# An attention and expert kernel: one written list for all engines, three score banks, output by transposition

## The chip, the cores and the metric

The kernel runs on one core of one Trainium2 chip. The metric is device time in microseconds, from a median of several runs. The core has five engines that matter here, each with its own instruction queue, executed in order: TensorE (PE in the profile; its weight loads have a lane of their own, PEld), VectorE (DVE), ScalarE (ACT), GpSimd (POOL), and SyncE (SP), which issues most DMA. TensorE writes only to PSUM, which has eight banks of 128 x 512 float32; DVE and ACT read it.

## The reference, cut to what matters

```python
# attention: B=8, H=8, S=576, D=64, window 128, per head an ALiBi slope
scores = q @ k.T / 8 + slope[h] * -(i - j)      # kept where 0 <= i - j < 128, else -1e9
attn   = exp(scores - max); attn /= sum + 1e-9
x      = (attn @ v) as (4608 tokens, 512)
# experts: N=4608, D=512, E=8, F=1024, capacity 576 tokens each
logits = x @ w_gate                             # 512 x 8
# tokens are assigned greedily in order of falling logit, 576 to each expert
out[mask_e] = relu(x[mask_e] @ w1[e]) @ w2[e]
```

## The kernel before, in words

The program has two stages. Attention fills the first 215 us of the span, the router and the eight experts the rest. The change touches attention alone.

Attention works on 32 pairs of heads (`NPAIRS = B * NP`, four pairs a batch of 576 tokens). Queries go in blocks of 64, and two neighbouring blocks and the two heads of the pair share a unit `t`, so a pair has five units, 0 to 4, the last a half one. Units 2 and 3 make up "half 0" of the scores, units 0, 1 and 4 "half 1" (`UNITS`). Even batches start their blocks at another place than odd ones: `unit()` gives unit 0 two key blocks and unit 4 three in even batches, and three and one in odd ones. So rounds come in two kinds, four of one and four of the other.

A pair passes through these steps, all of whose instructions are kept in the order of the program text by `put`, on every engine:

- `scores(n, half)`: TensorE in 64 x 64 tiles writes q k of a half into two banks, one per head. Products in plain float32 take two passes, each with its own weight load.
- `least(n, half)`: DVE adds the bias, stores the weights' exponents to `u` and their minimum to `mn`.
- `exps(n, half)`: ACT takes the exponential in place and sums it to `sm`.
- `turn(n, t, ps)`: TensorE transposes `u` into a bank (128 x 128, one pass; unit 4 is done with 64 x 64 products and goes into unit 0's bank); `turned` copies the bank to `PT0` to `PT3`, by ACT (units 2 and 0) or DVE (1 and 3).
- `av(n)`: TensorE in 64 x 64 tiles makes the transposed output x in two banks.
- `copy_out(n)`: ACT copies them to `xT`; POOL adds 1e-9 to the sums (`sd`).
- `natural(n, N)`: for each of five 128-token groups one product of `xT` (as weights, 128 x 128) with `wn`, which has 144 columns: an identity of 128 that turns x to token-major, and 16 gate columns, for the logits.
- `divide(n, N)`: DVE takes the reciprocal of the sums, then for each of two banks multiplies the 16 columns into `Lp` (`shares`) and the 128 into `xb` (`output`); SP stores `xb`; once a batch `logits` adds on POOL.

The loop runs 36 rounds. Round n works on five pairs at once: in TensorE's order it turns units 2, 1, 3 of pair n-2, makes `natural` of pair n-4, turns units 0 and 4 of pair n-2, makes `scores(n, 0)`, `av(n-3)` and `scores(n, 1)`. Between them `router.early_step` puts small pieces of the router (TensorE and DVE).

PSUM is split by pools: `ps_s` two banks (scores), `ps_t` four (turned weights and `natural`), `ps_x` two (`av`). A bank is given out in turn, and its next writer waits for the last reader of what was in it. A round takes four score banks: each half waits for `least` of the other half to have read both.

In the text below T0 to T4, S0, S1, A and N stand for TensorE's part of those steps, M for an instruction of `least`, E of `exps`, P0 to P3 for the copies of `turned`, X for the copies of `copy_out`.

Of the kernel before, what the change touches and what calls it, by code (L numbers as in the profile page):

```python
# [21 lines left out]
LAG = 2  # L22
UNITS = (2, 3), (0, 1, 4)
QKW, BMW, XW = 1152, 1216, 144


def attention(tc, pools, qk_in, v_in, rel_in, C, x_dram, L_sb, router):
# [18 lines left out]
    ident, wn = C["ident"], C["wn"]  # L46
# [59 lines left out]

    def scores(n, half):
        st = state[n]
# [12 lines left out]
        st["s"] = s  # L121

    def least(n, half):

        st = state[n]
        s = st["s"]
        for t in UNITS[half]:
            for h in range(2) if t < 4 else (0,):
                m, c, _, y = unit(n, t)
                y += 512 * h  # L130
                i = 2 * t + h
                u = weights(n, t, h)
                for rows, x in ((slice(0, 128), s[h]),) if t < 4 else ((hs[0], s[0]), (hs[1], s[1])):
                    put(nc.vector.tensor_tensor_reduce(out=u[rows], in0=x[rows, c:c + 64 * m].rearrange("q (j k) -> q j k", k=64),  # L134
                                                       in1=bm[n % NP][rows, y:y + 64 * m].rearrange("q (j k) -> q j k", k=64),
                                                       scale=-0.125, scalar=3e38, op0=ALU.add, op1=ALU.min,
                                                       accum_out=st["mn"][rows, i:i + 1]))

    def exps(n, half):
        st = state[n]  # L140
        for t in UNITS[half]:
            for h in range(2) if t < 4 else (0,):
                i = 2 * t + h
                u = weights(n, t, h)
                put(nc.scalar.activation(u, u, AF.Exp, bias=st["mn"][:, i:i + 1], scale=-1.0, accum_out=st["sm"][:, i:i + 1]))  # L145
# [5 lines left out]
    def turn(n, t, ps):  # L151

        u = state[n]["u"]
        m, _, o, _ = unit(n, t)
        for j in range(m):
            c = place(n, t, j)
            if t < 4:
                put(nc.tensor.transpose(ps[:, c:c + 128], u[:, o + 128 * j:o + 128 * j + 128], ident))  # L158
            else:
                for h in range(2):  # L160
                    mm(ps[hs[h], c:c + 64], u[hs[h], o + 64 * j:o + 64 * j + 64], ident[hs[h], hs[h]])

    def turned(n, t, ps, copy):
        T = state[n][t] = sb.tile([128, 576], F32, name=f"PT{t}")
        w = 384 if t else place(n, 4, unit(n, 4)[0])
        put(copy(T[:, 0:w], ps[:, 0:w]))
# [43 lines left out]
    def copy_out(n):  # L210
        st = state[n]
        xT = st["xT"] = sb.tile([128, 576], F32, name="xT")
        for i, w in ((0, 320), (1, 256)):
            put(nc.scalar.copy(xT[:, 320 * i:320 * i + w], st["x"][i][:, 0:w]))
# [17 lines left out]
    def divide(n, N):  # L232

        b, p = divmod(n, NP)
        bb, par = divmod(b, 2)
        if p == 0:
            batch[b] = (sb.tile([128, 5, 512], F32, name="xb", bufs=2), sb.tile([128, 5, 8, 8], F32, name="Lp", bufs=2))
        xb, Lp = batch[b]
        s = sb.tile([128, 5, 2], F32, name="rs")
        put(nc.vector.reciprocal(s, state.pop(n)["sd"].rearrange("q (t h) -> q t h", h=2)))  # L240

        def views(i):
            t0, t1 = (0, 3) if i == 0 else (3, 5)
            return t0, t1, N[i][:, 0:XW * (t1 - t0)].rearrange("q (t c) -> q t c", c=XW)

        def shares(i):
            t0, t1, x = views(i)
            put(nc.vector.tensor_tensor(Lp[:, t0:t1, :, 2 * p:2 * p + 2].rearrange("q t e h -> q t h e"),
                                        x[:, :, 128:144].rearrange("q t (h e) -> q t h e", h=2),
                                        bc(s[:, t0:t1].unsqueeze(3), [128, t1 - t0, 2, 8]), ALU.mult))  # L250

        def output(i):
            t0, t1, x = views(i)
            if n < NPAIRS - 2:
                put(nc.vector.tensor_tensor(xb[:, t0:t1, 128 * p:128 * p + 128].rearrange("q t (h c) -> q t h c", h=2),
                                            x[:, :, 0:128].rearrange("q t (h c) -> q t h c", h=2),
                                            bc(s[:, t0:t1].unsqueeze(3), [128, t1 - t0, 2, 64]), ALU.mult))
            else:
                for t in range(t0, t1):
                    for h in range(2):  # L260
                        put(nc.scalar.mul(xb[:, t, 128 * p + 64 * h:128 * p + 64 * h + 64],
                                          x[:, t - t0, 64 * h:64 * h + 64], s[:, t, h:h + 1]))

        def store():
            c0, cs = 9 * bb + 5 * par, 9 * bb + 4
# [3 lines left out]
            if p == NP - 1:  # L269
                nc.sync.dma_start(x_dram[128 * cs + 64 * par:128 * cs + 64 * par + 64, :], xb[hs[par], 4, :])  # L270

        for i in range(2):
            shares(i)
            if n < NPAIRS - 2:
                output(i)
# [8 lines left out]
        else:  # L284
            store()

# [26 lines left out]
    def bank():  # L313
        return ps_t.tile([128, 512], F32, name="pt")

    for n in range(NPAIRS + LAG + 2):
# [4 lines left out]
        if n == 2:  # L321
            nc.sync.dma_start(wn, C["wn_in"])
# [4 lines left out]
        k = n - LAG  # L327
        turns, ends = 0 <= k < NPAIRS, 0 <= k - 2 < NPAIRS
        if ends:
            copy_out(k - 2)  # L330
        if 0 < n <= NPAIRS:
            least(n - 1, 1)
        if turns:
            ps = {}
            for t in (2, 1, 3):
                ps[t] = bank()
                turn(k, t, ps[t])
            turned(k, 2, ps[2], nc.scalar.copy)
        if 0 < n <= NPAIRS:
            exps(n - 1, 1)  # L340
        if turns:
            turned(k, 1, ps[1], nc.vector.tensor_copy)
            turned(k, 3, ps[3], nc.vector.tensor_copy)
            room = ps[3][:, 384:512]
        if k - 1 == NPAIRS - 1:
            av(k - 1)
        if ends:
            N = [bank(), bank()]
            natural(k - 2, N)
        if turns:  # L350
            ps = bank()
            turn(k, 0, ps)
            turn(k, 4, ps)
            turned(k, 0, ps, nc.scalar.copy)
        if n < NPAIRS:
            if ends:

                router.early_step(room)
            scores(n, 0)
            least(n, 0)  # L360
            exps(n, 0)
        if ends:
            divide(k - 2, N)
            if (k - 2) % NP == NP - 1 and k - 2 < NPAIRS - 1:
                logits((k - 2) // NP)
        if 0 <= k - 1 < NPAIRS - 1:
            av(k - 1)
        if n >= NPAIRS:
            for _ in range(1 if turns else 2):
                router.early_step(room if turns else bank()[:, 384:512])  # L370
        if n < NPAIRS:
            scores(n, 1)


def host_attn(inputs):
# [9 lines left out]
    wn = np.zeros((2, D, NP, 2, XW), np.float32)  # L385
    for c in range(2):
        for o in range(2):
            h = c ^ o
            for d in range(D):
                wn[c, d, :, o, D * h + d] = 1.0  # L390
            wn[c, :, :, o, 128 + 8 * h:136 + 8 * h] = g[:, h].transpose(1, 0, 2)
# [7 lines left out]
    for r in range(2):  # L399
# [5 lines left out]
        for p in range(NP):  # L405
            rel[r, :, 512 + p] = 2.0 ** -(2 * p + r + 1)
    return dict(qk=qk.reshape(B, NP, 128, QKW), v=np.ascontiguousarray(vv).reshape(B, NP, 128, NB * D),
                wn=wn.reshape(128, 2 * NP * XW),
# [848 lines left out]
def moe_attn_kernel(tc, qk, v, w1, w2, wn, rel, ident, cst, out):  # L1257
    nc = tc.nc
    with ExitStack() as es:
# [4 lines left out]
        C = dict(ident_in=ident, wn_in=wn, cst_in=cst)  # L1264
# [6 lines left out]
        with ExitStack() as ea:  # L1271
            P["pp"] = ea.enter_context(tc.tile_pool(name="pp", bufs=1))
            P["attn"] = ea.enter_context(tc.tile_pool(name="attn", bufs=2))
            for k, b in (("ps_s", 2), ("ps_t", 4), ("ps_x", 2)):
                P[k] = ea.enter_context(tc.tile_pool(name=k, bufs=b, space=PSUM))
            warm(tc, P, C)
            C["wn"] = P["pp"].tile([128, 2 * NP * XW], F32, name="wn_sb")
# [17 lines left out]
_INS = ["qk", "v", "w1", "w2", "wn", "rel", "ident", "cst"]  # L1295
# [23 lines left out]
```

## Time and profile before

| what | value |
|---|---|
| median of three runs | 683.64 us (681.84, 684.50, 683.64) |
| the profiled execution | 683.86 us, of which the span of the trace is 681.7 us |
| PE, PEld busy | 655.0 us (96%), 580.3 us (85%) |
| DVE, ACT, POOL busy | 468.5, 386.4, 134.2 us |
| granted TensorE clock | 0.985 on average |
| `scores` of pair 5 to pair 31 (26 rounds) | 31.83 to 198.16 us |

A line of the timeline has the start and the length in us, the engine, the line of the kernel, the operation, what it writes and reads, and how many instructions of that kind were merged. A matmul's length contains a fixed latency, so in a stream the starts tell more than the lengths. PE rows of line 54 are the helper `mm`: their tiles say which step they belong to (`s<-qk` scores, `x<-PT,v` A, `pt<-wn_sb,xT` N, `pt<-ident_sb,u` 64*64 is T4); line 158 is T0 to T3, line 134 M, 145 E, 166 P, 214 X, 248 and 255 `shares` and `output`.

### The profile page before, as it was taken

What the parts mean: (1) busy time and instruction counts of PE and PEld (TensorE: products, weight loads), DVE (VectorE), ACT (ScalarE), POOL (GpSimd) and SP (SyncE); (2) the same over time, 40 slices, a digit from 0 to 9 for tenths busy, and PEclk for the clock granted to TensorE, in tenths of its full rate; (3) what the DMA queues carried; (4) which work ended last, traced back from release to release, by engine and by line L of the source; (5) the groups of instructions that cost most, each with busy time, mean ns of one, the idle gap of its engine ahead of it and who ended that gap; (6) DMA issues with size and microseconds to landing.
All of it is one profiled execution on the core that took longest, in us unless ns stands there. A gap on an engine that the chain in (4) does not pass through costs nothing.

```text
span 681.7 us, 18901 instructions
## 1 busy us (share of the span) xinstructions
PE 655.0 (96%) x7152; PEld 580.3 (85%) x7152; DVE 468.5 (69%) x1985; ACT 386.4 (57%) x1091; POOL 134.2 (20%) x296
## 2 busy tenths in 40 slices
PE   7999999999996699999999999999999999999995
PEld 4998998998986399889779879989989989989985
DVE  5788888888887799979749879776756625423210
ACT  6998898898884162434224546455546645644210
POOL 4021121121121201421412124013014014011011
PEclk9999999999998699999999999999999999999999
DMA  8556566566532361814515736637546556421001
GB/s 304 155 180 203 180 181 205 178 185 201 179 101 76 99 220 53 295 39 155 178 47 198 191 115 214 130 100 228 111 116 201 137 119 201 124 70 39 1 25 50
DMA packets 58980, 98.65 MB, mean 145 GB/s; under 512 B 27648, under 2 KB 36992, under 8 KB 58880
## 3 DMA queue, kind: packets, MB, share of 16 engines
q1 hardware_dynamic: 52992, 78.48, 38.6%
q0 software_dynamic: 5888, 18.88, 8.4%
q8 instruction: 58, 0.95, 0.6%
q14 instruction: 42, 0.34, 0.2%
HBM read 72.57 MB, written 18.87 MB: 134 GB/s over the span
## 4 chain that ended last, share of the span: by engine, by line
PE 86%; DVE 8%; DMA 3%; issue 1%; ACT 1%; POOL 0%; SPq 0%; POOLq 0%; DVEq 0%; ACTq 0%
PE ph L1059 24%; PE po L1087 10%; PE po L1088 10%; PE s L54 9%; PE po L1090 8%; PE pt L54 7%; PE pt L158 7%; PE x L54 6%; DMA raw<-in_w_dram 2%; DVE hl L967 2%; DVE hlo L1069 1%; PE m L610 1%; DVE u L134 1%; PE pg L1000 1%; PE ph L984 1%
## 5 line engine op out<-in xcount | busy, mean ns | idle before, releaser
L1059 PE MATMUL ph<-xh,hl 128*128 128x288 f32 (+2 forms) x1024 | 188.3, 298 | 0.6 <-ACT hh L1064 0.5
L1059 PEld LDWEIGHTS ph<-xh,hl 128*128 128x128 f32 x1024 | 154.6, 189 | 2.1 <-ACT hh L1064 0.7
L145 ACT ACTIVATE u<-u,mn 128x192 f32<-128x192 f32 (+2 forms) x288 | 123.9, 433 | 24.5 <-DVE mn L134 24.5
L1087 PE MATMUL po<-hl,hh 128*128 128x512 f32 (+1 forms) x328 | 128.3, 391 | 0.0
L1088 PE MATMUL po<-hl,hh 128*128 128x512 f32 (+1 forms) x328 | 126.2, 385 | 0.0
L1059 PE MATMUL ph<-xl,hl 128*128 128x288 f32 (+2 forms) x512 | 115.5, 297 | 0.0
L134 DVE CUSTOM_DVE_ANT_0 u<-s,bm 128x192 f32<-128x192 f32 x308 | 86.5, 333 | 30.0 <-PE s L54 29.2
L1064 ACT ACTIVATE hh<-ph 128x288 fp32r<-128x288 f32 (+2 forms) x128 | 46.5, 408 | 106.3 <-PE ph L1059 103.1
L1090 PE MATMUL po<-hl,hlo 128*128 128x512 f32 (+1 forms) x264 | 101.3, 384 | 0.0
L967 DVE TENSOR_TENSOR hl<-raw,hl 128x512 fp32r<-128x512 f32 x128 | 85.1, 684 | 22.0 <-ACT hl L965 21.6
L1099 POOL DMA_INDIRECT out_dram<-o,idx x40 | 42.2, 1056 | 274.9 <-ACT o L1094 216.0
L1059 PEld LDWEIGHTS ph<-xl,hl 128*128 128x128 f32 x512 | 84.1, 189 | 0.2 <-DVE xl L1038 0.2
L965 ACT CAST hl<-raw 128x1024 fp32r<-128x1024 f32 x64 | 65.9, 1051 | 22.1 <-DMA raw<-in_w_dram 17.7
L54 PE MATMUL s<-qk 64*64 64x192 f32 (+1 forms) x1112 | 69.7, 319 | 1.9 <-DVE mn L134 1.6
L1069 DVE SCALAR_TENSOR_TENSOR hlo<-ph,hh 128x288 fp32r<-128x288 f32 (+2 forms) x128 | 49.1, 416 | 32.5 <-ACT hh L1064 31.9
L1087 PEld LDWEIGHTS po<-hl,hh 128*128 128x128 f32 x328 | 61.8, 188 | 11.2
L1088 PEld LDWEIGHTS po<-hl,hh 128*128 128x128 f32 x328 | 61.7, 188 | 11.3
L1094 ACT COPY o<-po 128x512 f32<-128x512 f32 (+1 forms) x33 | 18.9, 573 | 91.0 <-PE po L1090 80.8
L1090 PEld LDWEIGHTS po<-hl,hlo 128*128 128x128 f32 x264 | 49.7, 188 | 9.9
L158 PE MATMUL pt<-ident_sb,u 128*128 128x128 f32 x368 | 54.2, 282 | 1.4 <-DVE mn L134 1.0
L54 PEld LDWEIGHTS s<-qk 64*64 64x64 f32 x1112 | 48.3, 132 | 8.1 <-issue 2.5
L145 ACT ACTIVATION_READ_ACCUMULATOR u<-u,mn 128x1 f32 x288 | 54.4, 189 | 0.0
(240 smaller groups left out, 902.6 us busy)
## 6 DMA issues: line engine op xcount, KB each, us to landing
raw<-in_w_dram SPq DMA_DIRECT2D x64, 512.0 KB, 4.3
qk<-in_qk_dram SPq DMA_DIRECT2D x32, 576.0 KB, 5.1
v<-in_v_dram SPq DMA_DIRECT2D x32, 288.0 KB, 3.6
x<-xb SPq DMA_DIRECT2D x14, 512.0 KB, 3.5
x<-xb SPq DMA_DIRECT2D x8, 128.0 KB, 3.2
x<-xb SPq DMA_DIRECT2D x4, 256.0 KB, 2.3
g<-x,idx POOLq DMA_INDIRECT x40, 3.8
out_dram<-o,idx POOLq DMA_INDIRECT x40, 2.8
```

Of the source, the lines that this page charges most:

```text
L54: put(nc.tensor.matmul(out, w, a, start=start, stop=stop, skip_group_check=True))
L134: put(nc.vector.tensor_tensor_reduce(out=u[rows], in0=x[rows, c:c + 64 * m].rearrange("q (j k) -> q j k", k=64), in1=bm[n % NP][rows, y:y ...
L145: put(nc.scalar.activation(u, u, AF.Exp, bias=st["mn"][:, i:i + 1], scale=-1.0, accum_out=st["sm"][:, i:i + 1]))
L158: put(nc.tensor.transpose(ps[:, c:c + 128], u[:, o + 128 * j:o + 128 * j + 128], ident))
L965: self.last = nc.scalar.copy(hl[:, 0, :], raw)
L967: nc.vector.tensor_tensor(hl[:, 1, c:c + 512], raw[:, c:c + 512], hl[:, 0, c:c + 512].bitcast(F32), ALU.subtract)
L1059: nc.tensor.matmul(pp[t], w[:, a, j, fo:fo + 128], x[:, j, cut[t]:cut[t + 1]], start=(i == 0), stop=(i == 11))
L1064: self.acted = nc.scalar.activation(o, pp[t], AF.Relu)
L1069: nc.vector.scalar_tensor_tensor(d, pp[t][:, c0:c1], 0.0, o[:, c0:c1].bitcast(F32), ALU.max, ALU.subtract)
L1087: nc.tensor.matmul(out, a, wh, start=(f == 0), stop=False)
L1088: nc.tensor.matmul(out, a, wl, start=False, stop=(f == 7 and t == 4))
L1090: nc.tensor.matmul(out, hl[:, f, 128 * t:128 * t + 128], wh, start=False, stop=(f == 7))
```

## The change

The order of a round is written out in one list, `ROUND`, whose entries are a step, its unit or half, and how many rounds back its pair started. The list orders each engine's work; instructions of different engines still wait only for data and buffers. `least`, `exps`, `turn`, `turned`, `copy_out`, `natural` and `divide` now do one unit, half or parity per call. Read by engine, the list is:

- PE: T0, S0, A, T4, S1, (router), T2, N odd, T1, N even, T3
- ACT: E00, E20, E40, E21, P3, E10, X1, E11, X0, E30, E01, P1, E31
- DVE: M11, D even, M30, M20, M21, reciprocal, (router), P0, M31, M01, P2, D odd, M10, M00, M40
- POOL: the sums (G)

The score pool has three banks and the pool of turned weights three. The turning goes by 128 x 128 transposition in `natural`, and a product with 16 columns (`wg`) makes the logits; groups are taken by the parity of t, and odd ones have their two heads swapped, so that `output` of the odd groups takes two instructions. P0 and P2 are on DVE, P1 and P3 on ACT. `sums` and the reciprocal are steps of their own. The last pair's `av` follows its P0 at once.

```diff
-LAG = 2
 UNITS = (2, 3), (0, 1, 4)
-QKW, BMW, XW = 1152, 1216, 144
+QKW, BMW, XW, GW = 1152, 1216, 144, 16
+ROUND = [(w[0], w[1:-2], int(w[-1])) for w in (
+    "T0-2 S0-0 E00-1 M11-1 De-4 E20-1 E40-1 G-2 A-3 E21-1 M30-0 P3-2 E10-1 M20-0 M21-0 X1-3 I-3 E11-1 T4-2 S1-0 R-0 T2-1 P0-2 "
+    "M31-0 X0-3 M01-0 No-3 E30-0 T1-1 P2-1 E01-0 Do-3 M10-0 M00-0 M40-0 P1-1 Ne-3 T3-1 E31-0").split()]
+ROUNDS = 4
...
-        s = [bank() if half and n < 2 else ps_s.tile([128, 512], F32, name="s") for _ in range(2)]
+        s = st["s", half] = [bank() if half and n == 0 else ps_s.tile([128, 512], F32, name="s") for _ in range(2)]
...
-    def turn(n, t, ps):
+    def turn(n, t):
+        ps = state[n]["pt", t % 4] = state[n]["pt", 0] if t == 4 else bank()
...
-    def turned(n, t, ps, copy):
+    def turned(n, t):
+        copy = nc.scalar.copy if t % 2 else nc.vector.tensor_copy
+        put(copy(T[:, 0:w], state[n]["pt", t][:, 0:w]))
+        if t == 0 and n == NPAIRS - 1:
+            av(n)
...
-    def natural(n, N):
-        for t in range(5):
-            w = xT[:, places[t]:places[t] + 128]
-            c = 2 * (n % NP) + t % 2
-            mm(N[t // 3][:, XW * (t % 3):XW * (t % 3) + XW], w, wn[:, XW * c:XW * c + XW])
+    def natural(n, par):
+        par = "eo".index(par)
+        N = state[n]["N", par] = bank()
+        g = GW * (2 * (n % NP) + par)
+        for i, t in enumerate(range(par, 5, 2)):
+            w = xT[:, places[t]:places[t] + 128]
+            put(nc.tensor.transpose(N[:, XW * i:XW * i + 128], w, ident))
+            mm(N[:, XW * i + 128:XW * i + XW], w, wg[:, g:g + GW])
...
+            elif a == 0:
+                put(nc.vector.tensor_tensor(xb[:, ts, 128 * p:128 * p + 128].rearrange("q t (h c) -> q t h c", h=2), ...
             else:
+                for h in range(2):
+                    put(nc.vector.tensor_tensor(xb[:, ts, 128 * p + 64 * h:128 * p + 64 * h + 64],
+                                                x[:, :, 64 - 64 * h:128 - 64 * h],
+                                                bc(s[:, ts, h:h + 1], [128, m, 64]), ALU.mult))
...
+        if par:
+            return
         (store and logits as before, after the even groups)
...
+    def route(n):
+        for _ in range(1 if n < NPAIRS + 2 else 2):
+            if n >= 4:
+                router.early_step(state[n - 2]["pt", 3][:, 384:512] if n < NPAIRS + 2 else bank()[:, 384:512])
+    for n in range(NPAIRS + ROUNDS):
+        (loads as before; wg, 128 columns, in place of wn, 1152)
+        for what, which, back in ROUND:
+            k = n - back
+            if what == "R":
+                route(n)
+            elif 0 <= k < NPAIRS:
+                ...
-            for k, b in (("ps_s", 2), ("ps_t", 4), ("ps_x", 2)):
+            for k, b in (("ps_s", 3), ("ps_t", 3), ("ps_x", 2)):
```

More of the change, by code (lines that the diff above doesn't have):

```diff
@@ L120, in scores, with least @@
                 mm(s[h][hs[r], c:c + w], q[hs[h], 64 * qb:64 * qb + 64], k[hs[h], 64 * kb:64 * kb + w])
-        st["s"] = s
-    def least(n, half):
+    def least(n, which):
+        t, h = int(which[0]), int(which[1])
         st = state[n]
[L126 to L137, printed above, removed]
@@ L139, in exps @@
-    def exps(n, half):
-        st = state[n]
[L141 to L145, printed above, removed]
+        s = st["s", int(t not in UNITS[0])]
+        m, c, _, y = unit(n, t)
+        y += 512 * h
+        i = 2 * t + h
+        u = weights(n, t, h)
+        for rows, x in ((slice(0, 128), s[h]),) if t < 4 else ((hs[0], s[0]), (hs[1], s[1])):
+            put(nc.vector.tensor_tensor_reduce(out=u[rows], in0=x[rows, c:c + 64 * m].rearrange("q (j k) -> q j k", k=64),
+                                               in1=bm[n % NP][rows, y:y + 64 * m].rearrange("q (j k) -> q j k", k=64),
+                                               scale=-0.125, scalar=3e38, op0=ALU.add, op1=ALU.min,
+                                               accum_out=st["mn"][rows, i:i + 1]))
@@ L208, in av, with copy_out, sums @@
                     mm(out, w, a, i == 0, i == len(todo[hc]) - 1)
[L210 removed]
+    def copy_out(n, i):
         st = state[n]
[L212 to L214 removed]
+        i = int(i)
+        if "xT" not in st:
+            st["xT"] = sb.tile([128, 576], F32, name="xT")
+        c, w = ((0, 320), (320, 256))[i]
+        put(nc.scalar.copy(st["xT"][:, c:c + w], st["x"][i][:, 0:w]))
+    def sums(n):
+        st = state[n]
         st["sd"] = sb.tile([128, 10], F32, name="sd")
@@ new lines, in output @@
+        def output(a):
+            ts, m, x = views(a)
+            if n >= NPAIRS - 2:
+                for i in range(m):
+                    t = a + 2 * i
+                    for h in range(2):
+                        o = 64 * (h ^ a)
+                        put(nc.scalar.mul(xb[:, t, 128 * p + 64 * h:128 * p + 64 * h + 64], x[:, i, o:o + 64], s[:, t, h:h + 1]))
+            elif a == 0:
+                put(nc.vector.tensor_tensor(xb[:, ts, 128 * p:128 * p + 128].rearrange("q t (h c) -> q t h c", h=2),
@@ L269, in store @@
             if p == NP - 1:
[L270 to L275, printed above, removed]
+                nc.sync.dma_start(x_dram[128 * cs + 64 * odd:128 * cs + 64 * odd + 64, :], xb[hs[odd], 4, :])
+        shares(par)
+        if n < NPAIRS - 2:
+            output(par)
+        if par:
+            return
         if n == NPAIRS - 2:
@@ L311, in attention, with values @@
     biases(0)
-    def bank():
-        return ps_t.tile([128, 512], F32, name="pt")
-    for n in range(NPAIRS + LAG + 2):
+    def values(n):
+        if n < NPAIRS - 1:
+            av(n)
+    def route(n):
+        for _ in range(1 if n < NPAIRS + 2 else 2):
+            if n >= 4:
+                router.early_step(state[n - 2]["pt", 3][:, 384:512] if n < NPAIRS + 2 else bank()[:, 384:512])
+    work = dict(S=scores, M=least, E=exps, T=turn, P=turned, X=copy_out, N=natural, D=divide)
+    alone = dict(A=values, G=sums, I=inverse)
+    for n in range(NPAIRS + ROUNDS):
         if 0 < n < NPAIRS - 1:
@@ L326, in attention @@
             biases(n)
[L327 to L372, printed above, removed]
+        for what, which, back in ROUND:
[3 more added lines that the diff above has]
+            elif 0 <= k < NPAIRS:
+                if what in alone:
+                    alone[what](k)
+                else:
+                    work[what](k, which)
 def host_attn(inputs):
```

75 lines of the change are left out of this document (41 added, 34 removed).

## The prediction

> **What bounds the kernel now.** I read the page first (busy shares, slices), then busy time by stage, then TensorE's timeline of one round of each kind.
>
> ```profile
> span 681.7 us, 18901 instructions
> PE 655.0 (96%) x7152; PEld 580.3 (85%) x7152; DVE 468.5 (69%) x1985; ACT 386.4 (57%) x1091; POOL 134.2 (20%) x296
> PEclk9999999999998699999999999999999999999999
> 6.00:31.83 25.83, 22.70 (x428) 19.03 (x428) 21.35 (x123) 23.56 (x100) 8.39 (x29) 1.00 0.73 246
> 31.83:198.16 166.33, 166.21 (x3430) 150.07 (x3426) 136.70 (x736) 144.30 (x575) 32.05 (x154) 1.00 0.59 182
> ```
>
> The last two lines are start:end, length, and busy time of PE, PEld, DVE, ACT and POOL (the stretches run from the first scores to those of pair 5, and from there to those of pair 31). In the second PE is busy 166.21 of 166.33 us: 26 rounds at 6.40 us, bound by TensorE, with DVE at 82% (5.26 a round) and ACT at 87% (5.55). In the first, ACT leads. But a busy PE is not one at its peak, so its own timeline decides.
>
> ```profile
> 111.33 1.20 PE L158 MATMUL pt<-ident_sb,u 128*128 128x128 f32 x9
> 112.37 1.39 PE L54 MATMUL pt<-wn_sb,xT 128*128 128x144 f32 x10
> 113.70 0.44 PE L158 MATMUL pt<-ident_sb,u 128*128 128x128 f32 x2
> 114.06 0.51 PE L54 MATMUL pt<-ident_sb,u 64*64 64x64 f32 x10
> 114.46 0.82 PE L54 MATMUL s<-qk 64*64 64x192 f32 x14
> 115.05 1.56 PE L54 MATMUL x<-PT,v 64*64 64x64 f32 x64
> 116.53 1.37 PE L54 MATMUL s<-qk 64*64 64x128 f32 x20
> 117.83 0.55 PE L158 MATMUL pt<-ident_sb,u 128*128 128x128 f32 x3
> ...
> 143.30 1.20 PE L158 MATMUL pt<-ident_sb,u 128*128 128x128 f32 x9
> 144.34 1.39 PE L54 MATMUL pt<-wn_sb,xT 128*128 128x144 f32 x10
> 145.64 0.55 PE L158 MATMUL pt<-ident_sb,u 128*128 128x128 f32 x3
> 146.11 0.27 PE L54 MATMUL pt<-ident_sb,u 64*64 64x64 f32 x2
> 146.83 1.60 PE L54 MATMUL x<-PT,v 64*64 64x64 f32 x64
> 148.34 1.26 PE L54 MATMUL s<-qk 64*64 64x192 f32 x20
> 149.54 0.33 PE L158 MATMUL pt<-ident_sb,u 128*128 128x128 f32 x1
> ```
>
> From start to start, an even batch's round is T2, T1, T3 1.04, N 1.33, T0 0.36, T4 with S0 0.99, A 1.48, S1 1.30: 6.50 us. An odd one's is 1.04, 1.30, 0.47, 0.72, 1.51, 1.20: 6.24. Mean 6.37. Two of these hold waits. The first is S1's:
>
> ```profile
> 115.46 0.36 DVE L134 CUSTOM_DVE_ANT_0 u<-s,bm 128x192 f32<-128x192 f32 x1 [1.35 <-PE s L54]
> 116.30 0.35 DVE L134 CUSTOM_DVE_ANT_0 u<-s,bm 128x192 f32<-128x192 f32 x1
> 116.49 0.19 PEld L54 LDWEIGHTS s<-qk 64*64 64x64 f32 x2
> 116.77 0.77 PEld L54 LDWEIGHTS s<-qk 64*64 64x64 f32 x18
> ```
>
> With two score banks, S1 may write only when the four M of S0 (first and last shown, 115.46 to 116.65) have read both banks. Two of its 20 loads go at 116.49, the other 18 at 116.77. The second is N's and T0's:
>
> ```profile
> 112.26 1.28 PEld L54 LDWEIGHTS pt<-wn_sb,xT 128*128 128x128 f32 x10
> 113.69 0.20 PEld L158 LDWEIGHTS pt<-ident_sb,u 128*128 128x128 f32 x2
> L158 PEld LDWEIGHTS pt<-ident_sb,u 128*128 128x128 f32 x287 | 30.4, 140 | 7.6 <-issue 3.3
> L54 PEld LDWEIGHTS pt<-wn_sb,xT 128*128 128x128 f32 x250 | 32.0, 190 | 0.0
> L54 PEld LDWEIGHTS s<-qk 64*64 64x64 f32 x900 | 39.3, 132 | 3.7 <-PE x L54 0.2
> L452 PEld LDWEIGHTS pt<-ed,craw 2*128 2x128 f32 x2 | 0.3, 182 | 0.1
> 197.85 0.29 PEld L452 LDWEIGHTS pt<-ed,craw 2*128 2x128 f32 x2
> ```
>
> N's ten loads follow each other by (1.28 - 0.19) / 9 = 0.121 us, so N could take 1.21, and T0 starts late, at 113.69, since its bank waits for a copy.
>
> **The change part by part.**
>
> N. It loses ten passes of 144 columns (1.31 us a round as it stands) and gains, for each of five groups, one transposition and two passes of 16 columns. In the streams above a transposition takes 0.109 (1.04 for nine, with a slow first one). A 16-column pass is new. Its matmul is short, and what remains is the load of 128 float32 columns. Weight loads last 190 ns with 128 columns, 132 with 64, 140 in a transposition: so 64 columns more are 58 ns more, the load itself some 0.11 us, and that of a transposition some 0.055. The nearest row for a load with almost no matmul behind it is the router's `ed` product, two loads of 128 columns and two-column matmuls in 0.29 us: they follow each other by 0.29 - 0.18 = 0.11. Per group: the first load hides behind the transposition (0.109), the second is bare (0.11), the next transposition's load is bare (0.055): 0.275, and five make 1.38. Bounds: at best a short pass costs no more than the 0.055 of a fast load, 5 x (0.109 + 0.11) = 1.10; at worst nothing hides, 5 x (0.109 + 0.11 + 0.11 + 0.055) = 1.92. I take 1.38, as loads run under matmuls throughout the N rows. Against 1.31 this alone costs 0.07.
>
> The Trainium skill (TensorE: Matmul & The Clock Gate, Back-to-back issue gap) gives a warm matmul N / 2.4 + 2.5 ns with a floor of about 25; on that alone N would be 5 x (0.109 + 0.05) = 0.80 and the round 0.6 shorter than I say. The two-column passes spaced by 0.11 speak against that formula here and for the same page's LDWEIGHTS section, by which a load takes columns / 1.2 whatever the rows, 107 ns.
>
> Score banks, two to three. The first bank of S0 now waits for the M of the round before; S1's first for M11 of this round, its second for M30 and M20 of S0. M30 can begin 0.4 after A's first pass (115.46 against 115.05) and two take 0.56 (three steps from 115.46 to 116.30), so both banks are free 1.0 after S0; S1 comes after A and T4, 1.5 to 1.8 after it. The wait goes. Free, S1 has six passes in its busiest quadrant: in S0 14 passes take 0.59 over four quadrants, 0.17 each for 192 columns, so 0.11 for 128 and 0.06 for 64. An even round has 2 x 0.11 + 4 x 0.17 = 0.90, an odd one 0.68 + 0.12 = 0.80; with 0.1 of change back to 128 x 128 (T0 streams to 113.70 + 0.055 + 2 x 0.109 = 113.97, T4 starts at 114.06) 1.00 and 0.90. It saves 0.30 in both.
>
> Split of T4 from T0. S0 now starts cold in the 64 x 64 tiles: 0.70 alone (the router round at 198.16 has it so, below), and T4 in the stream 0.30 or 0.08: 1.00 and 0.78, against 0.99 and 0.72. T0 no longer waits: 0.31 and 0.42 against 0.36 and 0.47.
>
> ```profile
> 198.16 0.88 PE L54 MATMUL s<-qk 64*64 64x192 f32 x16
> 198.86 0.60 PE L54 MATMUL x<-PT,v 64*64 64x128 f32 x15
> ```
>
> Sum of a round on PE: even 1.04 + 1.38 + 0.31 + 1.00 + 1.47 + 1.00 = 6.20; odd 1.04 + 1.38 + 0.42 + 0.78 + 1.50 + 0.90 = 6.02. Mean 6.11, against 6.37: 0.26 less.
>
> ```profile
> 111.97 0.48 ACT L166 COPY PT<-pt 128x384 f32<-128x384 f32 x1
> L166 DVE COPY PT<-pt 128x384 f32<-128x384 f32 x50 | 25.5, 552 | 0.8
> ```
>
> Three banks for turned weights and N. Six are taken a round, each waiting for the reader of the third before it: T0 for P1, T2 for D even, N odd for P3, T1 for P0, N even for P2, T3 for D odd. I followed a round from T2's first pass at 0. P2 can start at 0.64 (as the copy after 111.33 began at 111.97) and takes 0.55, free at 1.25 with 0.05 to the next load; N even is due at 0.38 + 0.55 + 0.33 = 1.26, and its first load, no longer ahead, costs 0.055. This one is just met. D odd ends at about 1.8, T3 is due at 2.1. P0 (DVE) ends near 6.0, T1 is due at 7.0. P1 ends at 2.0, T0 is due at 2.4. Since P2 has no slack and router pieces (0.4 to 0.65 of DVE, in half the rounds) stand ahead of P0, M31, M01 and P2, I put 0.06 a round for new waits; bounds 0 and 0.25 (a late P2 in full).
>
> DVE and ACT.
>
> ```profile
> L166 ACT COPY PT<-pt 128x448 f32<-128x448 f32 x25 | 13.3, 532 | 3.1 <-PE pt L54 2.2 <-ACT u L145 0.3
> L255 DVE TENSOR_TENSOR xb<-pt,rs 128x256 f32<-128x256 f32 x26 | 10.7, 413 | 0.0
> ```
>
> DVE gets the 448-column copy for one of 384 (64 / 384 of the 0.55 above, at most 0.09) and the odd output as two of 128 columns for one of 256 (one fixed part more, 0.1): 5.26 + 0.19 = 5.4 of 6.1. ACT loses 0.05: 5.5. Both hide behind PE, with 0.6 to spare; if that cover went, all of the 0.26 would be gone at 0.8 more. In DVE's queue M30 waits for S0 with M20, M21, the reciprocal and P0 behind it; P0 for T4; M01 for S1; P2 for T2.
>
> The rest. POOL's sums go two rounds earlier and wait for exponentials of the round before; the four logits adds stay behind them. D even's store follows the loads of its round on SP, as before. `wg` is 65 KB for 590 KB, behind the startup loads. `early_step` now follows the even groups' logits in the same round. I put these at nothing; ACT and PE cover them.
>
> Start and end. The same PE work stands ahead of pair 5's scores. What sets them is ACT (23.56 of 25.83).
>
> ```profile
> 7.36 0.46 ACT L145 ACTIVATE u<-u,mn 128x192 f32<-128x192 f32 x1 [5.34 <-DVE mn L134]
> 7.82 0.44 ACT L145 ACTIVATE u<-u,mn 128x192 f32<-128x192 f32 x1
> ```
>
> From 7.36 on, 36 exponentials at 0.44 (15.8) and seven copies at some 0.35 (2.4; they overlap, so less than the 0.53 of one above) allow T2 of pair 3 at 25.6, and S0 of pair 5 2.7 later, at 28.3 against 31.83. Bounds 0 and 3.5; I take 2.0, since queues in order do not keep ACT full. At the end the last N comes one round earlier, but takes longer and stands behind a lone chain P0, A, X, N as before: 0, bounds -1 and +1.
>
> **Sum.** 26 x (0.26 - 0.06) = 5.2, start 2.0, end 0: 7.2 us. The profiled execution took 683.86 (span 681.7 and 2.2 around it), 0.03% above the median of 683.64. Forecast 676.5.
>
> **Rivals.**
>
> No new wait, full start: 26 x 0.26 + 3.5 = 10.3, so 673.5 or less. For it, the hand-followed round closes without a wait; against it, P2's slack of 0.01.
>
> The bank wait comes back elsewhere: 0.25 a round at N even or S0 and a start of 0.5: 683.86 - 26 x 0.01 - 0.5, about 683, no change. For it, one bank fewer for six users; against it, only P2 is tight.
>
> DVE becomes the bound (slower). Its queue holds 5.4 us and four waits for PE in order. If each wait costs the 0.3 us that a consumer needs after its producer and none overlaps work, a round is 5.4 + 4 x 0.3 = 6.6, 0.2 above today's: 26 x 0.23 = 6, so 690. It decides from 1.0 us of waits a round on. Against it: I find 0.75.
>
> The clock. Transpositions rise from 11.5 to 16.5 a round and stand in one stretch of 2.8 us with little else. If the chip did not count them as work and halved the clock there, a round would cost 2.8 more, 26 x 2.8 = 73, so 750. Every slice of attention shows full clock with the 11.5. The Trainium skill (same page, PE-mode transpose) says that transpositions do not count as PE-busy; this trace does not bear that out so far.
>
> **How the numbers follow.** About 0.5% (3.4 us) is what can be told from no change. Forecast, 673.5 to 680.2: 0.57. No new wait, below 673.5: 0.18. Bank wait back, 680.2 to 687: 0.15. Slower: DVE 0.08, clock 0.02. So faster 0.75, same 0.15, slower 0.10. The range runs from 671 (a start better by 3.5, N at 1.30) to 685 (0.25 a round, no gain at the start, 1 lost at the end); the forecast's own is 673.5 to 680.
>
> **What would show it.** Right: rounds of 6.0 to 6.25 us between scores; S1's 20 loads unbroken behind T4; 15 loads a pair for N, 0.275 a group; DVE and ACT near 89%. Wrong: gaps of PE before N even, S1 or S0 of over 0.1 us with DVE named; a 16-column pass spaced by more than 0.15 or less than 0.08; scores of pair 5 later than 31 us.

## The result, and the profile after

The changed kernel takes 687.50 us (median) where the kernel before takes 683.64: the ratio is 1.006, with a 95% interval of 1.0036 to 1.0083. The forecast was 676.5, faster; it is slower by 0.6%, a little more than can be told from no change. One of its seventeen runs took 727.73 us at a mean granted clock of 0.839 and stands outside the ratio. The profiled execution took 684.53 us and is one of its quickest; the median lies 3 us above it, which needs an explanation of its own below.

The page's head, and busy time by stage (start:end, length, then busy time of PE, PEld, DVE, ACT, POOL, granted clock, DMA share), with the same borders as in the prediction: first scores, scores of pair 5, scores of pair 31, the last sum of logits, the end. The last fence is the kernel before in the two stages that the prediction did not show.

```profile
span 682.7 us, 19282 instructions
PE 651.0 (95%) x7312; PEld 579.0 (85%) x7312; DVE 474.9 (70%) x2015; ACT 383.7 (56%) x1091; POOL 135.9 (20%) x296
```

```profile
6.00:32.47 26.47, 22.55 (x428) 18.93 (x427) 22.00 (x126) 21.83 (x92) 9.37 (x34) 1.00 0.68 216
32.47:196.63 164.16, 160.80 (x3558) 147.66 (x3557) 143.43 (x772) 141.52 (x574) 32.20 (x154) 1.00 0.59 185
196.63:218.25 21.62, 17.70 (x402) 16.27 (x401) 13.13 (x66) 12.91 (x52) 3.42 (x14) 1.00 0.18 58
218.25:682.70 464.45, 445.19 (x2917) 394.62 (x2917) 295.15 (x1050) 206.12 (x376) 90.12 (x89) 0.97 0.43 128
```

```profile
198.16:215.88 17.72, 16.66 (x378) 15.47 (x377) 14.03 (x70) 11.19 (x42) 4.26 (x19) 1.00 0.25 74
215.88:681.70 465.82, 444.69 (x2917) 394.22 (x2917) 295.24 (x1050) 206.03 (x376) 88.70 (x89) 0.98 0.43 128
```

Stage by stage against the kernel before: start 26.47 against 25.83, 0.64 longer (forecast: 2.0 shorter); 26 rounds 164.16 against 166.33, 2.17 shorter (forecast 5.2); the drain from the scores of pair 31 to the last logits 21.62 against 17.72, 3.90 longer (forecast 0); behind it 464.45 against 465.82. The sum is the 1.0 by which the spans differ. In the second stage PE is now idle for 3.4 us where it was idle for 0.1.

An undisturbed round did what was forecast. TensorE's timeline over an even round (T2, odd N, T1, even N, T3 with T0, S0, A, T4, S1) up to the next T2 and S0, and one row of its weight loads:

```profile
128.28 0.55 PE L168 MATMUL pt<-ident_sb,u 128*128 128x128 f32 x3
128.66 0.27 PE L255 MATMUL pt<-ident_sb,xT 128*128 128x128 f32 x1
128.77 0.29 PE L61 MATMUL pt<-wg_sb,xT 128*128 128x16 f32 x2
...
129.20 0.53 PE L168 MATMUL pt<-ident_sb,u 128*128 128x128 f32 x3
129.56 0.30 PE L255 MATMUL pt<-ident_sb,xT 128*128 128x128 f32 x1
129.71 0.29 PE L61 MATMUL pt<-wg_sb,xT 128*128 128x16 f32 x2
129.85 0.31 PE L255 MATMUL pt<-ident_sb,xT 128*128 128x128 f32 x1
129.99 0.29 PE L61 MATMUL pt<-wg_sb,xT 128*128 128x16 f32 x2
130.13 0.31 PE L255 MATMUL pt<-ident_sb,xT 128*128 128x128 f32 x1
130.28 0.29 PE L61 MATMUL pt<-wg_sb,xT 128*128 128x16 f32 x2
130.42 0.74 PE L168 MATMUL pt<-ident_sb,u 128*128 128x128 f32 x5
131.09 0.88 PE L61 MATMUL s<-qk 64*64 64x192 f32 x16
131.79 1.53 PE L61 MATMUL x<-PT,v 64*64 64x128 f32 x68
133.15 0.45 PE L61 MATMUL pt<-ident_sb,u 64*64 64x64 f32 x9
...
134.37 0.55 PE L168 MATMUL pt<-ident_sb,u 128*128 128x128 f32 x3
...
137.29 0.88 PE L61 MATMUL s<-qk 64*64 64x192 f32 x16
...
133.44 0.86 PEld L61 LDWEIGHTS s<-qk 64*64 64x64 f32 x18
```

The round takes 134.37 - 128.28 = 6.09 us; the eight from 88.68 to 137.29, one full pattern of odd and even batches, mean 6.08. N takes 1.40 (128.66 to 129.20 and 129.56 to 130.42), S1's loads go unbroken, and no stage waits. At 6.08 the 26 rounds would be 158.0. So 6.2 us were lost on top of rounds that are better than forecast, and the two ends lost more.

Four places show it. First, DVE at the start: a cast of constants (L1150, `load_consts` at round `CONST_AT` = 4) waits for their DMA, with P2's copy (L178) and the rest of the queue behind it.

```profile
18.68 0.23 DVE L1150 CAST c_ones<-craw 128x128 bf16<-128x128 f32 x1 [1.51 <-DMA craw<-in_cst_dram]
18.82 0.55 DVE L178 COPY PT<-pt 128x384 f32<-128x384 f32 x1
```

Second, the two rounds before pair 31, in which the router step R has TensorE work (L460). The list puts R behind S1 on TensorE but ahead of P0 on DVE. TensorE's rows, then DVE's:

```profile
191.78 0.38 PE L460 MATMUL pt<-ed,craw 2*128 2x2 f32 x2
...
193.98 0.52 PE L168 MATMUL pt<-ident_sb,u 128*128 128x128 f32 x3 [0.77 <-DVE PT L178]
195.00 0.30 PE L255 MATMUL pt<-ident_sb,xT 128*128 128x128 f32 x1 [0.50 <-ACT u L153]
...
192.19 0.16 DVE L460 COPY ev<-pt 128x2 f32<-128x2 f32 x1 [1.48 <-PE pt L460]
...
193.22 0.62 DVE L178 COPY PT<-pt 128x448 f32<-128x448 f32 x1
```

DVE stands 1.48 us until S1 and the router's product are through, does seven small operations and only then P0 (193.22), whose bank T1 needs (193.98). The rounds to the scores of pairs 30 and 31 take 7.45 and 7.90: 3.2 us lost.

Third, the drain, where the same order holds P0 of pair 31, and with it A of that pair (212.08), by 2.04 us; then N's even half waits 1.14 us for a bank that the outputs of pair 30 on ACT (L286) still hold, since three banks now serve what four did.

```profile
209.48 0.57 PE L460 MATMUL pt<-OH,ind 128*128 128x16 bf16 x13
212.08 1.57 PE L61 MATMUL s<-PT,v 64*64 64x128 f32 x64 [2.04 <-DVE PT L178]
...
216.90 0.33 PE L255 MATMUL pt<-ident_sb,xT 128*128 128x128 f32 x1 [1.14 <-ACT xb L286]
...
210.15 0.16 DVE L460 COPY pt<-pt 64x8 f32<-64x8 f32 x1 [2.07 <-PE pt L460]
...
211.40 0.62 DVE L178 COPY PT<-pt 128x448 f32<-128x448 f32 x1
```

Fourth, there are three breaks of TensorE for which the profile names no wait ("issue"), in dense stretches of passes in 64 x 64 tiles: two in T4, one in S1. Rounds with them took 7.07, 6.74 and 7.06: some 2.3 us more than like rounds. TensorE's timeline, then the DMA queues in the microsecond from 82.2 on:

```profile
83.67 0.22 PE L61 MATMUL pt<-ident_sb,u 64*64 64x64 f32 x1
84.50 0.45 PE L61 MATMUL pt<-ident_sb,u 64*64 64x64 f32 x8 [0.61 <-issue]
```

```profile
q8 instruction: 1, 0.02, 5.9%
```

A packet of the queue q8 (16 KB), whose kind is "instruction" in the profile, starts at 82.24 and takes 0.94; TensorE goes on 1.3 us after its end. The page has 59 such packets (0.97 MB) for TensorE's 14,624 loads and passes. In the trace of the kernel before there is no such break between pair 5 and pair 31.

### The profile page after: what moved, and what is told of

Same layout as the page of the kernel before. It is cut to its first block, busy times and chain, and to the rows that moved or that the text cites. A ratio compares the mean times of both kernels' runs of the same rounds, so it can differ in the third digit from the quotient of the medians.

```text
span 682.7 us, 19282 instructions
## 1 busy us (share of the span) xinstructions
PE 651.0 (95%) x7312; PEld 579.0 (85%) x7312; DVE 474.9 (70%) x2015; ACT 383.7 (56%) x1091; POOL 135.9 (20%) x296
## 4 chain that ended last, share of the span: by engine, by line
PE 85%; DVE 11%; issue 2%; DMA 1%; ACT 0%; SPq 0%; POOL 0%; POOLq 0%; DVEq 0%
PE ph L1067 25%; PE po L1095 10%; PE po L1096 10%; PE po L1098 8%; PE s L61 8%; PE pt L168 6%; PE x L61 6%; PE pt L61 4%; PE pt L255 3%; DVE hl L975 2%; DVE hlo L1077 1%; PE ph L992 1%; DMA craw<-in_cst_dram 1%; PE m L618 1%; PE pg L1008 1%
## 5 line engine op out<-in xcount | busy, mean ns | idle before, releaser
L153 ACT ACTIVATE u<-u,mn 128x192 f32<-128x192 f32 (+2 forms) x288 | 125.5, 438 | 13.8 <-DVE mn L143 13.5
L143 DVE CUSTOM_DVE_ANT_0 u<-s,bm 128x192 f32<-128x192 f32 (+1 forms) x314 | 93.8, 333 | 9.6 <-PE s L61 6.6
L61 PE MATMUL s<-qk 64*64 64x192 f32 (+1 forms) x1132 | 65.0, 321 | 2.6 <-DVE mn L143 2.5
L168 PE MATMUL pt<-ident_sb,u 128*128 128x128 f32 x368 | 59.4, 283 | 2.3 <-DVE PT L178 2.2
L984 POOL DMA_INDIRECT g<-x,idx x40 | 41.6, 1041 | 67.8 <-issue 33.4
```

Source lines behind the costliest of these rows:

```text
L61: put(nc.tensor.matmul(out, w, a, start=start, stop=stop, skip_group_check=True))
```

## The experiments

The theories: the *queue theory* (the router step's, the casts' and the last bank's places hold TensorE), against the *clock theory* (the loss sits in half-clock stretches); for the breaks without a wait the *fetch theory* (TensorE uses its instructions up faster than they are fetched). All ratios are to the kernel before on the same chip; the changed kernel's is 1.006.

**Router step between P0 and S1.**

```
-T4-2 S1-0 R-0 T2-1 P0-2 M31-0 ...
+T4-2 P0-2 R-0 S1-0 T2-1 M31-0 ...
```

> Router step R moved in the list from behind S1 to between P0 and S1 (on TensorE ahead of S1, on DVE behind P0). Queue theory (router pieces ahead of P0 on DVE, with their TensorE part only behind S1, hold the rounds in which the router has TensorE work): the two rounds before the scores of pair 31 fall from 7.45 and 7.90 us to 6.6 or less each, the 2.04 us of TensorE before A of pair 31 go, the last logits sum comes 3.5 to 5 us earlier than 218.25, and the time is 3 to 5 us below the changed kernel, about 683. Clock theory (the loss sits behind attention, in the stretch at half clock): the rounds shorten, but the time stays within 1 us of the changed kernel's 687.5.

Ratio 1.0046 (1.0029 to 1.0064), 1 us better than the changed kernel instead of 3 to 5, and within its interval. The mechanism showed: the rounds before pair 31 fell to 6.56 and 6.83, and A of pair 31 waits 0.73 for P0 instead of 2.04. But the steps without TensorE work, harmless ahead of P0, now delay M31, M01 and P2, which has no slack:

```profile
50.42 0.30 PE L255 MATMUL pt<-ident_sb,xT 128*128 128x128 f32 x1 [0.26 <-ACT u L153]
...
49.73 0.55 DVE L178 COPY PT<-pt 128x384 f32<-128x384 f32 x1
```

The row names ACT; by the order in which banks are given out, even N's bank comes free with P2's end (49.73 + 0.55 = 50.28). Six rounds lose 0.4 so, and don't with the router step ahead of P0 again (below). The casts also waited 3.1 us in this profile, instead of 1.5.

**Casts later.** The DMA stays at round 4; `eb`, `ones`, `low` are cast in round 6, the others in round 8.

```
+CASTS = {6: ("eb", "ones", "low"), 8: ("i64", "h10", "cc")}
+        for c in CASTS.get(n, ()):
+            casts[c]()
```

> The DMA of the constants is issued where it was, but DVE's casts of them stand two and four rounds later. Queue theory (DVE waits 1.5 us for that DMA with P2 and M behind it): no wait of DVE on it, scores of pair 5 at 30.7 to 31.2 instead of 32.47, the time 1.3 to 1.8 us below the changed kernel. Clock theory, or a start set by ACT alone: scores of pair 5 earlier by less than 0.5, time unchanged.

Ratio 1.0028 (1.0007 to 1.0048), 2.2 us better than the changed kernel. DVE no longer waits for the constants, and the scores of pair 5 come at 30.57: 1.9 earlier, and 1.26 earlier than in the kernel before.

**A score bank for the last N.**

```
-        N = state[n]["N", par] = bank()
+        N = state[n]["N", par] = ps_s.tile(..., name="s") if n == NPAIRS - 1 and par == 0 else bank()
```

> The even N of the last pair takes an idle score bank instead of one of the three turned-weight banks. Queue theory (it waits 1.14 us for a bank that the outputs of pair 30 still hold on ACT): the last logits sum 1.1 us earlier than 218.25, time 1.0 to 1.2 below the changed kernel. Clock theory: time unchanged within what can be told.

Ratio 1.0018 (0.9992 to 1.0043): better than the changed kernel, and the wait on L286 is gone from the trace (N of pairs 30 and 31 runs unbroken from 218.88 to 222.05). How much of it is the bank can't be told, since its profile shows something else: a break without a wait in S1, behind it N's transpositions, and then half clock. TensorE's timeline, then three-microsecond windows:

```profile
153.35 0.37 PE L61 MATMUL s<-qk 64*64 64x192 f32 x1 [1.31 <-issue]
```

```profile
153.00:156.00 3.00, 2.65 (x19) 2.42 (x20) 2.06 (x11) 1.26 (x5) 0.00 (x0) 0.82 0.48 156
156.00:159.00 3.00, 3.00 (x22) 2.46 (x26) 1.43 (x8) 2.68 (x13) 0.00 (x0) 0.50 0.43 163
159.00:162.00 3.00, 3.00 (x81) 2.92 (x77) 1.05 (x7) 0.00 (x0) 0.75 (x4) 0.54 0.30 106
```

From 154.9 to 161.8 the granted clock is 0.5; the two rounds there took 9.14 and 7.75, 4.9 us more than like rounds, the break included. This profiled execution took 689.74 at a mean clock of 0.975. The changed kernel's runs lie at 0.973 to 0.979 in 12 of 16 (688.7 us on average) and at 0.982 or 0.983 in the other four, the profiled one among them (685.5 us); half the runs of the kernel before lie at 0.985 or above.

**All three.**

> The three edits together (router step between P0 and S1, casts later, score bank for the last N). Queue theory: they add up, 5.5 to 8 us below the changed kernel, 679.5 to 682, so below the kernel before (683.6) as well; last logits sum at 210.5 to 213. Clock theory: less than 2 us of it arrives at the end.

Ratio 0.9982 (0.9963 to 1.0001), 5.3 us better than the changed kernel and level with the kernel before. None of the three alone is clear of the changed kernel's interval; together they are. They add up, just below the range. The last logits came at 217.99, not 210.5 to 213, since the six rounds of 0.4 and breaks without a wait (2.3 us of TensorE's idle time put down to "issue" between pairs 5 and 31) are still in it, and since the drain still takes 20.3 us against 17.7 in the kernel before: TensorE waits 2.2 us there for copies and exponentials, and the trace of the kernel before names no such wait there.

**N by products of 144 columns**, on top of the three.

```
-            put(nc.tensor.transpose(N[:, XW * i:XW * i + 128], w, ident))
-            mm(N[:, XW * i + 128:XW * i + XW], w, wg[:, g:g + GW])
+            mm(N[:, XW * i:XW * i + XW], w, wg[:, g:g + GW])      # GW = 144: identity and 16 columns
```

> On top of the three edits, N again by products of 144 columns with a matrix that holds the identity and the 16 columns: no transposition and no short pass. By the prediction's term (1.31 against 1.38 a round) a round is 0.07 us shorter, 2 us in all; by the trace of the changed kernel (0.28 a group, 1.40 a round, against 1.21 to 1.25 for ten loads spaced by 0.121 to 0.125) 0.15 to 0.19, 4 to 5.5 us in all. Fetch theory beside it: 10 instructions of TensorE a round fewer, so no more breaks than before. If the 16-column form is the cheaper one instead, the rounds get longer.

Ratio 0.9953 (0.9936 to 0.9969). Like rounds fell from 6.10, 6.20, 5.97 and 6.06 to 6.02, 6.13, 5.89 and 5.99: 0.08 a round, the prediction's 0.07 and not the 0.15 to 0.19 of the other reading. So the transposition with 16 columns is the dearer form.

**Two score banks, four for turned weights**, on top of the three.

```
-("ps_s", 3), ("ps_t", 3)      M20-0 M21-0 X1-3 ...   M31-0 behind S1
+("ps_s", 2), ("ps_t", 4)      M20-0 M21-0 M31-0 X1-3 ...
```

> On top of the three edits, banks as in the kernel before: two for scores, four for turned weights, and M31 behind M21. By the prediction's term S1 waits 0.30 a round again, and S0's second bank now also waits for M11 by up to 0.3: 0.3 to 0.6 a round, 8 to 18 us more than the three edits alone. If three score banks had been worth nothing: unchanged. Fetch theory: S1's wait lets the instruction fetch catch up, so fewer breaks of TensorE without a wait, which gives up to 3 us back.

Ratio 1.0153 (1.0128 to 1.0178), some 12 us slower than the three edits: its rounds mean 6.55, and S0 is held in its middle. And no break without a wait is left, as in the kernel before, which fits the fetch theory: waits in the dense stretch give the instructions time to arrive.

**T2 between A and T4**, on top of the three.

```
-I-3 E11-1 T4-2 P0-2 R-0 S1-0 T2-1 M31-0 ... T1-1 P2-1 ...
+I-3 E11-1 T2-1 P2-1 T4-2 P0-2 R-0 S1-0 M31-0 ... T1-1 ...
```

> On top of the three edits, T2 (and its copy P2) stands between A and T4 instead of behind S1, so that the dense stretch of 64-column passes is cut by three 128 x 128 ones. Fetch theory (TensorE runs dry because its instructions are used up faster than fetched there): the breaks without a wait, 3.6 us in the profile of the three edits, fall to 1 or less; 2 to 3 us faster, about 680. If the breaks are of another kind (a wait that the trace does not name): they stay, and the time is within 1 us of the three edits, 682.9, or above it if P2 in its new place holds P0 back.

Ratio 1.0046 (1.0021 to 1.0071): a miss. Named idle without a wait fell from 2.3 to 1.3 us, as the fetch theory has it but by less than it said, and each round grew by some 0.25 (6.36 and 6.23 instead of 6.10 and 5.97), which ate that up. In an even round of this trace the step from A's first pass to the next stage takes 1.47 instead of 1.35 and T2 0.48 instead of 0.38, both at places where TensorE now changes once more between 64 x 64 and 128 x 128 tiles; that fits the 0.1 that the prediction had for such a change.

**Sixty passes at the start**, on top of the three.

```
+        if n == 2:
+            z = bank()
+            for _ in range(60):
+                mm(z[0:64, 0:64], ident[0:64, 0:64], ident[0:64, 0:64])
```

> On top of the three edits, sixty passes of 64 columns stand in TensorE's idle time at the start (round 2), which shifts its instructions by 120 places against the fetches of 256. Fetch theory: the breaks without a wait move to other rounds or stages and change in number (0 to 5 us in all), while all other waits stay. If the breaks belong to the rounds (a semaphore, a transfer of x): they stay in the rounds where the three edits have them, before scores of pairs 13, 25 and 27.

Ratio 1.0086, since the passes cost 7.2 us at the start (scores of pair 3 at 25.19 instead of 17.96). The breaks moved: in the three edits they stand ahead of the scores of pairs 14, 25, 26, 27 and 28, here of 15, 28 and 29, and in other stages. They belong to a place in TensorE's instruction stream.

The traces say more. Number TensorE's rows of a trace (loads, passes and the few of its sequencer) from 0 in order of time. In all sixteen traces instruction 256 n + 193 begins at least 1.20 us after the end of the n-th packet of q8, in each of 896 cases. The instruction just ahead of it begins earlier than that in 53 cases of 900, once 0.23 us before the packet has ended. And each of the 37 breaks of over 0.3 us that the passes show without a named wait, between pairs 5 and 31, stands at instruction 256 n + 193 or 256 n + 194, in every kernel that has such breaks, the one with the sixty passes included. So TensorE waits there for the n-th packet: the breaks are late fetches.

**Router step ahead of S1 and of P0.** With the casts later and the score bank:

```
-T4-2 S1-0 R-0 T2-1 P0-2 ...
+T4-2 R-0 S1-0 T2-1 P0-2 ...
```

> Casts later and score bank for the last N as in the three edits, but the router step stands ahead of S1 on TensorE and still ahead of P0 on DVE. Queue theory: the steps without TensorE work fall back into DVE's idle time ahead of P0, so the 0.4 us that six rounds of the three edits lose between T1 and N go (2.4 us), the steps with TensorE work lose at most 0.6 a round; last logits sum 1.5 to 3 us earlier than the 217.99 of the three edits, ratio to before 0.993 to 0.996 against their 0.998. If P0's place is what counts and not TensorE's: as the changed kernel in the two rounds before pair 31 (7.4 and 7.9), no gain over the three edits.

Ratio 0.9983 (0.9963 to 1.0002), no better than the three edits. The six rounds are back at 5.96 to 6.20, and the two before pair 31 take 6.68 and 7.15. But A of pair 31 waits 2.04 for P0 again, and in this profile the clock fell to half behind that wait, so that the last logits came at 219.93. A break of 1.21 us in S1, at the place of the one of 1.31 in the run with the score bank alone and with the same transpositions behind it, left the clock at 1.00 here.

**The same with N by products.**

> The run before with N by products of 144 columns. From the product run: regular rounds 0.08 shorter, 2 to 2.5 us less, fewer breaks without a wait; ratio to before 0.988 to 0.993. If the gain of the product run came from its breaks' chance places: the same as the run before.

679.41 us against 684.10: ratio 0.9936 (0.9914 to 0.9957), better than both kernels, just short of what was expected. Three stages of it:

```profile
6.00:30.57 24.57, 22.26 (x418) 18.43 (x417) 21.11 (x120) 21.67 (x92) 9.40 (x34) 1.00 0.77 255
30.57:192.30 161.73, 158.60 (x3429) 143.79 (x3428) 142.94 (x776) 141.31 (x574) 32.19 (x154) 1.00 0.60 187
192.30:213.68 21.38, 18.45 (x382) 16.86 (x381) 13.11 (x66) 12.05 (x48) 3.40 (x14) 0.92 0.19 58
```

It still has four breaks without a wait, in the same four consecutive rounds and ahead of the very same groups of passes as the other kernels with products have them. TensorE's timeline of this kernel, then of the last one below:

```profile
125.17 1.11 PE L61 MATMUL s<-qk 64*64 64x192 f32 x20 [1.18 <-issue]
131.83 0.39 PE L61 MATMUL pt<-ident_sb,u 64*64 64x64 f32 x7 [0.60 <-issue]
138.53 0.39 PE L61 MATMUL x<-PT,v 64*64 64x64 f32 x10 [0.49 <-issue]
```

```profile
124.44 1.11 PE L61 MATMUL s<-qk 64*64 64x192 f32 x20 [0.64 <-issue]
131.65 0.39 PE L61 MATMUL pt<-ident_sb,u 64*64 64x64 f32 x7 [1.15 <-issue]
138.63 0.39 PE L61 MATMUL x<-PT,v 64*64 64x64 f32 x10 [0.77 <-issue]
```

**Breaks on purpose**, with N by transpositions and with N by products (on the two kernels above).

```
+            for _ in range(4):
+                put(nc.gpsimd.tensor_scalar(z, state[n - 2][0][:, 0:320], 1.0, 1.0, ALU.mult, ALU.mult))
+            mm(state[n - 2]["pt", 3][0:64, 384:448], z[0:64, 0:64], ident[0:64, 0:64])
```

> TensorE is stopped on purpose in five rounds (10, 14, 18, 22, 26): behind T2 it waits for four POOL operations of 0.46 us that begin with P0, about 1.5 us, right ahead of N by transpositions. This adds work and leaves none out. Clock theory (a break of that length and the transpositions behind it let the clock fall to half, as behind the 1.64 us break at 151.7 in the bank run): stretches at half clock of about 6 us behind most of the five breaks, 3 us lost in each, 20 us slower in all. If the fall of the clock there was chance: full clock, 5 x 1.5 = 7.5 us slower.

> The same five breaks with N by products of 144 columns. If transpositions don't count as work for the clock: fewer half-clock stretches than with transpositions, 7.5 us slower than without breaks. If only the break counts: as many as there.

703.26 and 692.32 us, from two runs each: 19.9 and 12.9 above the kernels without breaks. The five breaks came to 8.8 and 9.2 us together, more than the 7.5 planned. The break of round 14 is the same in both (2.1 us behind T2); windows behind it, with transpositions, then with products:

```profile
95.00:98.00 3.00, 2.37 (x14) 2.31 (x15) 0.87 (x6) 0.10 (x1) 0.49 (x2) 0.66 0.37 143
98.00:101.00 3.00, 3.00 (x20) 2.60 (x21) 1.68 (x10) 3.00 (x13) 1.14 (x4) 0.50 0.00 1
```

```profile
93.00:96.00 3.00, 2.77 (x25) 2.48 (x26) 1.61 (x12) 1.29 (x6) 0.17 (x1) 1.00 0.21 84
96.00:99.00 3.00, 3.00 (x106) 2.88 (x105) 2.80 (x15) 2.81 (x13) 1.86 (x8) 1.00 0.44 154
```

With transpositions the clock fell behind all five breaks, for 3.4 or 6.8 us each and 27 us in all, with products behind two, for 3.4 us each; the times fit that. But five against two of five is few, and another wait gives the opposite count. TensorE's wait of 2.04 us ahead of A of pair 31, with the same work just in front of it, stands in eight of the profiles. The clock fell within 1.2 us of its end in all three with products, and in two of five with transpositions; in the changed kernel's own profile it did not. So breaks of this length can let the clock fall, and that the transpositions behind them decide it is not shown.

**N by products alone in the changed kernel.**

> The changed kernel with one part undone: N by products of 144 columns (the router step, the casts and the banks as changed). Clock theory (the typical run of the changed kernel is 3 us above its profiled one because transpositions behind a break let the clock fall): mean clocks of nearly all runs at 0.982 or above, against 0.973 to 0.979 in 12 of 16 of the changed kernel, and 2 us of shorter rounds: 4.5 to 6 us below it, ratio to before 0.997 to 1.000. If N's form only has its price of 0.08 a round: 2 us below, ratio 1.003, low clocks as often as before.

Ratio 1.0008 (0.9987 to 1.0030): 3.6 us below the changed kernel, between the two expectations. Six of twelve runs lie at a clock of 0.980 or less, where the clock theory had nearly all at 0.982 or above. So the form of N is worth its 2 us (the regular rounds are 0.08 shorter here too); whether the other 1.6 us are the clock's is not shown. The waits in the drain are still there, and the clock fell at one of them in this profile.

**Router step in two places**: ahead of P0 up to round 28, behind it from round 29 on.

```
+T4-2 R-0 P0-2 Q-0 S1-0 T2-1 ...
+            if what in "RQ" and (what == "Q") == (n >= 29): route(n)
```

> The run with the router step ahead of P0 and N by products of 144 columns, and from round 29 on, where the router step has TensorE work, it stands behind P0. Queue theory: the two rounds before pair 31 fall from 6.60 and 7.07 to 6.5 and 6.8, A of pair 31 comes 0.5 us earlier behind its scores and the last logits sum 1.5 us: ratio to before 0.990 to 0.992 instead of 0.9936. If P0 isn't what these rounds wait for: the same ratio.

Ratio 0.9928 (0.9903 to 0.9954). The two rounds before pair 31 take 6.49 and 6.76, the last logits come at 211.96 instead of 213.68, and A of pair 31 0.5 us earlier behind its scores, as expected; in the time it can't be told from the kernel with 0.9936.

## Why the prediction was wrong

- **N** was right in its sum: 0.28 a group and 1.40 a round against a forecast of 0.275 and 1.38, and 0.08 a round dearer than the product, measured by itself. Its parts were not: in most groups the transposition takes 0.14 to 0.15, where 0.109 had been put, and the two short passes 0.14 together, where it was 0.165, so two errors offset each other.
- **S1's wait** was right: gone, S1 at 0.88 to 0.98 (forecast 0.90 to 1.00). What it is worth alone was not separated: with two banks put back a round is 6.55 against 6.08, S0's wait included.
- **T4 apart from T0, and A**: 1.36 for A where 1.47 and 1.50 had been taken over from rounds in which it follows mixed work. The regular round is 6.08, not 6.11, and the new waits of 0.06 are not there.
- **"`early_step` now follows the even groups' logits in the same round. I put these at nothing; ACT and PE cover them."** This step failed. The cover holds for a step that is DVE work alone. Where its TensorE part stands behind S1 and its DVE part ahead of P0, DVE waits for S1, and P0, M31, M01 and P2 wait with it: 3.2 us in two rounds and 2.04 in the drain. The prediction had seen these pieces "ahead of P0, M31, M01 and P2" and had priced their length, not the wait inside them.
- **End: "0, bounds -1 and +1"** failed: 3.90. It followed the chain P0, A, X, N and left out the router step in its way (2.04) and the fourth bank that the last N had used (1.14). Of the other 0.7, 0.4 is a wait for an exponential on ACT; the rest stays open. With all three edits the drain is still 2.5 us longer than before.
- **Start: 2.0** failed: 0.64 lost. The scores of pair 5 could come 1.26 earlier (the run with later casts) and did not, since `load_consts` is tied to a round: DVE reaches its casts at 17.2 instead of 19.8, and their DMA lands at 18.6 (19.5 in the kernel before).
- **Breaks without a wait** were in no term: 2.3 us. The waits that the change took away had given TensorE's instructions time to arrive. That they are late fetches shows in their place: always the same one in a block of 256 instructions, 1.2 to 1.6 us behind the end of the packet of the same number, while sixty passes move them to other rounds and the kernels with S1's wait have none.
- **The clock rival**, put at 2 in 100 and 73 us, did not come in the form that was priced: the transpositions of undisturbed rounds run at a granted clock of 1.00. But behind a break the clock can fall to half for 3.4 or 6.8 us, which was in no term. The Trainium skill (TensorE: Matmul & The Clock Gate, PE-mode transpose) says that transpositions do not count as PE-busy in the same way; the breaks on purpose point that way (five of five against two of five), and the wait in the drain does not (two of five against three of three). The same page (HAM oscillation) warns of idle gaps above about 3.4 us; here gaps of 1.3 to 2.1 us were enough in some cases. Such falls would explain most of the 3 us between the changed kernel's profile and its median: the mean clocks fit (0.005 of 687 us is 3.4), its runs at the lower clocks are 3.2 us longer on average, and the profile of the run with the score bank shows such a stretch. But no profile of the changed kernel itself in that state was taken.

In numbers of the profiled execution: 166.33 - 158.0 = 8.3 us were gained in the rounds. 3.2 (router), 2.3 (breaks) and 0.7 (rest) were lost there again, 0.64 at the start and 3.9 at the end, where a gain of 2.0 and nothing had been put; behind attention 1.4 us were gained, which no term had.

## What to carry to other kernels

Where one list sets the order on all engines, follow each item that has work on two engines separately on each: a small step whose first half is queued late on one engine and whose second half is queued early on another makes everything behind the second wait for the first. Rounds that differ from the regular one (start, drain, rounds with extra work) need their own walk through the queues; here the regular round was forecast to 0.1 us, and the other places turned a gain into a loss. A wait that is taken away may have been covering something else: count what was done in its shadow, the arrival of instructions included.

## What was not expected of the hardware

- In stretches with 96 passes in 64 x 64 tiles in 2.6 us (A, T4, S1) TensorE stops for 0.3 to 1.7 us with no wait named, always at the same place in a block of 256 of its instructions, and resumes 1.2 to 1.6 us after the end of a 16 KB packet of its instruction queue.
- Breaks of 1.3 to 2.1 us of TensorE let the clock fall to half for 3.4 or 6.8 us in some cases and not in others: put in ahead of fp32 transpositions five times in five, ahead of products of 144 columns twice in five, and at the drain's wait of 2.04 us five times in eight.
- The constants' DMA, issued at the same place in the program, kept DVE waiting 0.3, 1.5 and 3.1 us in three kernels that share this code (N by products alone, the changed kernel, and the router step between P0 and S1).
